# Attention scores as row-tiled matmuls, with the block mask added by 32-row matmuls, in a fused block-sparse attention and MLP kernel

## The chip, the cores and the metric

The kernel runs on one core of one Trainium2 chip. The metric is the device time of the launch in microseconds (us); lower is better. A run that is over 1.5% longer than the fastest run of the same kernel counts as slow and is left out of ratios. Ratios are computed as the mean time of one kernel's fast runs over the mean time of the other kernel's fast runs of the same rounds, so they are not quite the ratio of the medians quoted beside them.

The engines in the profile are PE (TensorE matmul), PEld (TensorE weight load), DVE (VectorE), ACT (ScalarE), POOL (GpSimd) and SP (SyncE, which here issues transfers). "PEclk" is the share of the full TensorE clock that was granted. PE computes with an array of 128 rows by 128 columns; a matmul can use a part of it, a tile, and the profile prints that part as rows*columns ("64*128").

## The reference, cut to what matters

Inputs q, k and v have the shape (4, 8, 768, 64): batch, heads, positions, head size. The keys are cut into 24 chunks of 32. For every query an upper bound of its score with each chunk is computed, the 6 best chunks that causality allows are kept, and all other scores are masked.

```python
ub = np.sum(np.maximum(q * k_min, q * k_max), axis=-1)      # shapes cut
ub = np.where(causal, ub, -1e9)
top_chunks = np.argsort(ub, axis=-1)[..., -6:]
scores = scale * np.matmul(q, k.transpose(0, 1, 3, 2))
mask = sel & (pos[:, None] >= pos[None, :])                 # sel: chunk of the key is among the 6
attn = softmax(np.where(mask, scores, -1e9))
x = np.matmul(attn, v)                                      # heads side by side: 3072 x 512
h = x @ w_in                                                # 512 -> 2048
out = elu(h) @ w_out                                        # 2048 -> 512
```

## The kernel before: the parts that matter here

Heads are worked on in 16 pairs (4 batches of 4 pairs). Queries 0 to 191 need no mask, since they have at most 6 chunks (Q0 = 192). A head has 64 numbers per key, so a score matmul needs only 64 of the 128 rows of the array. The kernel before uses the other 64 rows for the mask: rows that hold -40000 on "not selected" chunks are multiplied with a 0/1 selection. Score and mask are thus one 128-row matmul per head. The price is that K and Q of each head are copied to their own tiles (64 partitions each), and that the transposed selection, selT, must be moved to other partitions by four transfers per two pairs.

```python
for s in range(NSET):                       # NSET = 4, pairs t use set t % 4
    lhsA.append(const.tile([P, S], BF16))   # rows 0-63: K of head 0, rows 64-87: mask values
    lhsB.append(const.tile([P, S], BF16))   # rows 64-127: K of head 1, rows 0-23: mask values
    rhsA.append(const.tile([P, S], BF16))   # rows 0-63: Q of head 0, rows 64-87: selection
    rhsB.append(const.tile([P, S], BF16))
...
# prep(t): after PE has transposed K (and Q, in the same way)
nc.scalar.activation(out=lhsA[s][0:64, ts], in_=ps[0:64, :], func=AF.Copy)
nc.scalar.activation(out=lhsB[s][64:P, ts], in_=ps[64:P, :], func=AF.Copy)
...
# select(g): upper bounds of two pairs, thresholds, transposed selection
nc.vector.transpose(out=selT, in_=sb...)
for j in range(2):
    s = (2 * g + j) % NSET
    nc.sync.dma_start(out=rhsA[s][64:64 + NCH, Q0:S], in_=selT[64 * j:64 * j + NCH, :])
    nc.sync.dma_start(out=rhsB[s][0:NCH, Q0:S], in_=selT[64 * j + 32:64 * j + 32 + NCH, :])
...
# attend(t): 7 steps a pair, 9 score matmuls a head
for hd in range(2):
    sps = psS.tile([P, 512], F32, name="sps")            # psS: 2 PSUM banks
    for (kb, c0, w, pc) in segs:
        nc.tensor.matmul(sps[:, pc:pc + w], lhsT=lhs[hd][:, P * kb:P * (kb + 1)],
                         rhs=rhs[hd][:, c0:c0 + w], start=True, stop=True)
    nc.scalar.activation(out=pt[:, hd, 0:wtot], in_=sps[:, 0:wtot], func=AF.Exp, scale=SCALE)
# (steps of at most 256 columns put both heads in one bank and one exponential)
```

A scheduler orders each engine's instructions when the program is built; the MLP of one batch is filled in between the attention of the next. In program order loads of later pairs stand ahead of the selection's transfers in the SP queue.

The softmax here doesn't subtract the row's maximum and nothing guards it: scores larger than these inputs give would overflow.

## Time and profile before

| | before |
|---|---|
| time, median of 3 runs | 397.43 us (396.59 to 397.96) |
| profiled execution, first to last instruction | 394.6 us |
| mean granted clock | 0.930 |
| PE / ACT / DVE / POOL busy | 317.5 / 226.5 / 205.0 / 116.2 us |

The first lines are from the page of the kernel before: busy time per engine, and then the span in 40 slices (about 10 us each), each digit the busy share in tenths; the last line is the granted clock in tenths.

```profile
PE 317.5 (80%) x2272; PEld 175.1 (44%) x2272; DVE 205.0 (52%) x594; ACT 226.5 (57%) x489; POOL 116.2 (29%) x244
...
PE   1562068678869869999998788999999988979886
...
ACT  2633086696896894785378956672589143251430
...
PEclk9995559959998989999999699999999999999999
```

PE has a hole in the fifth slice (the "0"), is 60 to 90% busy while attention dominates, and is nearly full from the middle on. The clock falls to half around the hole and in a few slices after it. The first digits of the clock line mislead: the trace's clock records begin only 25.0 us into this span, and the 9s before them stand for no record. The fp32 transposes there start 213 ns apart, against 109 ns later at full clock, so PE ran at half clock.

The hole, from the timeline of the kernel before. Columns: start in us, duration in us, engine, source line, operation, what it writes and reads, count, and in brackets the engine's idle time before it and what ended it. "SPq" is the issue of a transfer from the SP queue.

```profile
28.02 0.77 DVE L214 STREAM_TRANSPOSE selT<-selb_171 128x576 bf16<-128x576 bf16 x1
...
31.59 9.38 SPq L85 DMA_DIRECT2D q_pair<-in_q_dram  x2
41.07 5.13 SPq L82 DMA_DIRECT2D k_pair<-in_k_dram  x2
46.30 0.86 SPq L217 DMA_DIRECT2D rhsA_119<-selT  x1
...
49.00 0.58 PE L243 MATMUL sps<-rhsA_119,lhsA_117 128*128 128x384 bf16 x2 [15.38 <-DMA rhsA_119<-selT]
```

The selection is ready at 28.8 us, but its transfer stands behind loads of later pairs and is issued at 46.3 us; PE waits 15.4 us for it, and the first score comes at 49.0 us.

One more reading: what a change of tiling mode costs, that is, of the part of the array that matmuls use. The kernel before has 16 such changes, around the upper-bound matmuls (ub), which write 64 columns of the array ("128*64") between ordinary 128*128 matmuls. Timeline, PE only:

```profile
63.50 0.34 PE L284 MATMUL pxt<-ident_b,on 128*128 128x128 bf16 x3
63.77 0.46 PE L200 MATMUL ub<-QTf,kst_133 128*64 128x288 f32 x1
63.78 0.46 PE L200 MATMUL ub<-QTf,kst_139 128*64 128x288 f32 x1
```

The spacing of starts is what counts, not the printed duration: a 384-column matmul is printed with about 0.32 us, but the next one can start 0.162 us after it. The third transpose starts at 63.621 us by the trace's own records; its 128 columns take 56 ns when such matmuls stand back to back; the next start is 150 ns after it. So 92 to 94 ns are lost, in six of the seven selections of the steady part.

### The profile page before, as it was taken

How to read it: one execution, taken by the hardware profiler on the slowest of the kernel's cores; microseconds unless marked ns; L12 is line 12 of the kernel's file. 1: busy time of each engine (PE TensorE's matmuls, PEld its weight loads, DVE VectorE, ACT ScalarE, POOL GpSimd, SP SyncE). 2: the span in 40 equal slices, each digit the busy share in tenths (PEclk: the TensorE clock that was granted, in tenths of full speed). 3: DMA queues.
4: the chain of work that ended last, by engine and by line, in shares of the span. 5: the costliest groups of instructions: out<-in, count | busy, mean ns of one | idle time of the engine just before them, and what ended most of it. 6: DMA issues, size and time to landing. Idle time of an engine off the chain costs nothing.

```text
span 394.6 us, 6477 instructions
## 1 busy us (share of the span) xinstructions
PE 317.5 (80%) x2272; PEld 175.1 (44%) x2272; DVE 205.0 (52%) x594; ACT 226.5 (57%) x489; POOL 116.2 (29%) x244
## 2 busy tenths in 40 slices
PE   1562068678869869999998788999999988979886
PEld 1331034444544545554555454554556444444442
DVE  7462026637638737555286396372686345252550
ACT  2633086696896894785378956672589143251430
POOL 7651001201413322243033233251133134151430
PEclk9995559959998989999999699999999999999999
DMA  9999993543643733930233034101100010200102
GB/s 174 209 186 189 192 207 21 85 108 24 87 104 21 113 81 26 173 94 2 80 28 26 2 26 54 53 2 45 38 13 2 27 53 2 80 2 35 44 2 80
DMA packets 82592, 27.52 MB, mean 70 GB/s; under 512 B 76160, under 2 KB 78976, under 8 KB 82560
## 3 DMA queue, kind: packets, MB, share of 16 engines
q1 hardware_dynamic: 54784, 19.77, 20.4%
q0 software_dynamic: 27776, 7.34, 18.2%
q8 instruction: 18, 0.29, 0.3%
q14 instruction: 14, 0.11, 0.1%
HBM read 27.26 MB, written 6.29 MB: 85 GB/s over the span
## 4 chain that ended last, share of the span: by engine, by line
issue 30%; PE 24%; ACT 18%; POOL 16%; DVE 8%; SPq 3%; DMA 1%; POOLq 0%; ACTq 0%
POOL m_sb L301 13%; PE o_ps L308 9%; ACT pt L246 5%; PE sps L243 4%; PE ub L200 3%; DVE gT L303 2%; PE h_ps L295 2%; SPq L85 2%; PE psK L162 2%; PE psQ L182 2%; ACT QTf L187 1%; SPq L82 1%; ACT e_sb L299 1%; ACT rhsB_120 L189 1%; ACT lhsB_118 L169 1%
## 5 line engine op out<-in xcount | busy, mean ns | idle before, releaser
L295 PE MATMUL h_ps<-xt,w_in_sb 128*128 128x384 bf16 x512 | 105.3, 327 | 12.1 <-DVE gT L303 11.5
L301 POOL TENSOR_SCALAR m_sb<-e_sb 128x384 f32<-128x384 f32 x128 | 65.6, 516 | 155.2 <-ACT e_sb L299 143.8
L246 ACT ACTIVATE pt<-sps 128x384 bf16<-128x384 f32 (+1 forms) x160 | 80.4, 534 | 53.4 <-PE sps L243 51.5
L303 DVE SCALAR_TENSOR_TENSOR gT<-h_ps,m_sb 128x384 bf16<-128x384 f32 x128 | 70.4, 554 | 41.4 <-POOL m_sb L301 38.1
L308 PE MATMUL o_ps<-w_out_sb,gT 128*128 128x512 bf16 x384 | 88.1, 379 | 0.0
L299 ACT ACTIVATE e_sb<-h_ps 128x384 f32<-128x384 f32 x128 | 62.3, 496 | 40.4 <-PE h_ps L295 38.6
L295 PEld LDWEIGHTS <-w_in_sb 128*128 128x128 bf16 x512 | 48.3, 97 | 47.3 <-issue 20.2
L308 PEld LDWEIGHTS <-gT 128*128 128x128 bf16 x384 | 37.2, 98 | 40.8 <-issue 1.0
L314 DVE COPY o_sb<-o_ps 128x512 f32<-128x512 f32 x16 | 11.1, 691 | 53.1 <-PE o_ps L308 53.0
L273 PEld LDWEIGHTS <-pt 128*128 128x128 bf16 x672 | 29.3, 103 | 17.5 <-DVE pt L255 8.0
L182 PE MATMUL psQ<-ident_f,q_pair 128*128 128x128 f32 x96 | 21.0, 338 | 17.3 <-ACT lhsB_118 L169 7.3
L162 PE MATMUL psK<-ident_f,k_pair 128*128 128x128 f32 x96 | 19.2, 317 | 11.2 <-DMA k_pair<-in_k_dram 4.6
L312 ACT ACTIVATE o_sb<-o_ps 128x512 f32<-128x512 f32 x8 | 4.8, 597 | 39.0 <-PE o_ps L308 39.0
L190 DVE TENSOR_SCALAR Qrl<-QTf 128x576 f32<-128x576 f32 x16 | 7.5, 469 | 35.1 <-ACT QTf L187 35.1
L182 PEld LDWEIGHTS psQ<-ident_f,q_pair 128*128 128x128 f32 x96 | 12.3, 164 | 28.5 <-ACT lhsB_118 L169 10.1
L243 PE MATMUL sps<-rhsA_119,lhsA_117 128*128 128x384 bf16 (+2 forms) x36 | 9.9, 315 | 18.4 <-DMA rhsA_119<-selT 15.4
L255 DVE TENSOR_TENSOR pt<-pt,tri_168 128x512 bf16<-128x512 bf16 x32 | 13.5, 421 | 13.4 <-ACT pt L246 13.4
L162 PEld LDWEIGHTS psK<-ident_f,k_pair 128*128 128x128 f32 x96 | 11.5, 157 | 19.6 <-ACT rhsB_120 L189 5.6
L249 ACT ACTIVATE pt<-sps 128x512 bf16<-128x512 f32 x32 | 19.3, 604 | 1.4 <-PE sps L243 1.3
L285 DVE COPY xt<-pxt 128x384 bf16<-128x384 bf16 x32 | 11.3, 352 | 16.2 <-PE pxt L284 15.8
L165 DVE TENSOR_REDUCE kmm<-psK 128x12 f32<-128x384 f32 x32 | 17.6, 549 | 3.9 <-PE psK L162 3.4
L166 DVE TENSOR_REDUCE kmm<-psK 128x12 f32<-128x384 f32 x32 | 17.4, 545 | 0.0
(220 smaller groups left out, 418.2 us busy)
## 6 DMA issues: line engine op xcount, KB each, us to landing
k_pair<-in_k_dram SPq DMA_DIRECT2D x32, 192.0 KB
q_pair<-in_q_dram SPq DMA_DIRECT2D x32, 192.0 KB
out_dram<-o_sb SPq DMA_DIRECT2D x24, 256.0 KB
w_in_sb<-in_moe_w_in_dram POOLq DMA_DIRECT2D x4, 512.0 KB, 8.9
w_out_sb<-in_moe_w_out_dram POOLq DMA_DIRECT2D x4, 512.0 KB, 17.3
vext_116<-in_v_dram POOLq DMA_DIRECT2D x8, 96.0 KB, 3.4
vext_122<-in_v_dram POOLq DMA_DIRECT2D x8, 96.0 KB, 3.6
vext_128<-in_v_dram POOLq DMA_DIRECT2D x8, 96.0 KB, 3.4
```

The costliest lines, as they stand in the source:

```text
L162: nc.tensor.transpose(ps[:, P * n:P * (n + 1)], k_pair[:, 3 * h + n], ident_f)
L165: nc.vector.tensor_reduce(out=kmm[:, 0, cs], in_=pv, axis=AX.X, op=AOT.min)
L182: nc.tensor.transpose(ps[:, P * n:P * (n + 1)], q_pair[:, 3 * h + n], ident_f)
L243: nc.tensor.matmul(sps[:, o + pc:o + pc + w], lhsT=lhs[hd][:, P * kb:P * (kb + 1)], rhs=rhs[hd][:, c0:c0 + w], start=True, stop=True)
L246: nc.scalar.activation(out=pt[:, hd, 0:wtot], in_=sps[:, 0:wtot], func=AF.Exp, scale=SCALE)
L249: nc.scalar.activation(out=pt[:, :, 0:256], in_=sps[:, :].rearrange("p (h w) -> p h w", h=2), func=AF.Exp, scale=SCALE)
L273: nc.tensor.matmul(o3[:, hd, qi, :], lhsT=pt[:, hd, P * qt + off:P * qt + off + P], rhs=vexts[s][:, kb, hd, :], start=(kb == 0), stop=(kb ...
L295: nc.tensor.matmul(hw, lhsT=w_in_sb[:, kk, P * fc:P * (fc + 1)], rhs=xT[NPAIR * b + kk][:, ts], start=(kk == 0), stop=(kk == NKK - 1))
L299: nc.scalar.activation(out=e_sb, in_=hw, func=AF.Exp)
L301: nc.gpsimd.tensor_scalar(out=m_sb, in0=e_sb, scalar1=-1.0, scalar2=1.0, op0=AOT.add, op1=AOT.mult)
L303: nc.vector.scalar_tensor_tensor(out=gT[:, fc, :], in0=hw, scalar=0.0, in1=m_sb, op0=AOT.max, op1=AOT.min)
L308: nc.tensor.matmul(o_ps, lhsT=gT[:, fc, P * tt:P * (tt + 1)], rhs=w_out_sb[:, fc, :], start=(fc == 0), stop=(fc == NFC - 1))
```

## The change

The intent: use the array's rows for two heads at once. The score matmul of head 0 uses rows 0 to 63 and that of head 1 rows 64 to 127, so both could run side by side; K and Q are then copied once with all 128 partitions. The mask becomes a second, accumulating matmul over the 32 rows in which the transposed selection already lies, so that its transfers go.

```diff
-    ptpool = pool("ptpool", 14)
+    ktpool = pool("ktpool", 5)
+    ptpool = pool("ptpool", 10)
-    xtpool = pool("xtpool", 12)
+    xtpool = pool("xtpool", 10)
 ...                                      # set-up of lhsA, lhsB, rhsA, rhsB goes; emask = econst
-            nc.scalar.activation(out=lhsA[s][0:64, ts], in_=ps[0:64, :], func=AF.Copy)
-            nc.scalar.activation(out=lhsB[s][64:P, ts], in_=ps[64:P, :], func=AF.Copy)
+            nc.scalar.activation(out=kT[t][:, ts], in_=ps, func=AF.Copy)
 ...                                      # the same for Q
-                for j in range(2):
+                for i in range(4):
+                    h, j = divmod(i, 2)
                     t = 2 * g + j
-                    nc.tensor.matmul(ub[64 * j:64 * j + 64, :], lhsT=kst[t % NSET][:, w, :],
+                    nc.tensor.matmul(ub[32 * i:32 * i + 32, :], lhsT=kst[t % NSET][:, w, h, :],
 ...
-        for j in range(2):
-            s = (2 * g + j) % NSET
-            nc.sync.dma_start(out=rhsA[s][64:64 + NCH, Q0:S], in_=selT[64 * j:64 * j + NCH, :])
-            nc.sync.dma_start(out=rhsB[s][0:NCH, Q0:S], in_=selT[64 * j + 32:64 * j + 32 + NCH, :])
+        selT_of[g] = selT
 ...
+                spss = [psS.tile([P, 512], F32, name="sps") for _ in range(2)]
+                for (kb, c0, w, pc) in segs:
+                    m0 = max(c0, Q0)
+                    for hd in range(2):
+                        hr = slice(64 * hd, 64 * hd + 64)
+                        nc.tensor.matmul(spss[hd][:, pc:pc + w], lhsT=kT[t][hr, P * kb:P * (kb + 1)],
+                                         rhs=qT[t][hr, c0:c0 + w], start=True, stop=False)
+                    for hd in range(2):
+                        mr = slice(64 * hd + 32 * (t % 2), 64 * hd + 32 * (t % 2) + 32)
+                        nc.tensor.matmul(spss[hd][:, pc + m0 - c0:pc + w],
+                                         lhsT=emask[mr, P * kb:P * (kb + 1)],
+                                         rhs=selT[mr, m0 - Q0:c0 + w - Q0], start=False, stop=True)
                 for hd in range(2):
 ...                                      # the shared exponential of small steps goes
+                    nc.scalar.activation(out=pt[:, hd, 0:wtot], in_=spss[hd][:, 0:wtot],
                                          func=AF.Exp, scale=SCALE)
```

More of the change, by code (lines that the diff above doesn't have):

```diff
@@ L97 @@
     nc.vector.tensor_copy(out=ident_b, in_=ident_f)
-    vexts, lhsA, lhsB, rhsA, rhsB, kst = [], [], [], [], [], []
+    vexts, kst = [], []
     for s in range(NSET):
         vexts.append(const.tile([P, NQT, 2, D + 1], BF16, name=f"vext{s}"))
-        lhsA.append(const.tile([P, S], BF16, name=f"lhsA{s}"))
-        lhsB.append(const.tile([P, S], BF16, name=f"lhsB{s}"))
-        rhsA.append(const.tile([P, S], BF16, name=f"rhsA{s}"))
-        rhsB.append(const.tile([P, S], BF16, name=f"rhsB{s}"))
-        kst.append(const.tile([P, 2, 64], F32, name=f"kst{s}"))
+        kst.append(const.tile([P, 2, 2, CHUNK], F32, name=f"kst{s}"))
     def load_v(t):
@@ L116 @@
         nc.vector.memset(vexts[s][:, :, :, D:D + 1], 1.0)
-        nc.vector.memset(rhsA[s][64:P, :], 0.0)
-        nc.vector.memset(rhsB[s][0:64, :], 0.0)
     econst = const.tile([P, NCH, CHUNK], BF16, name="econst")
     nc.vector.memset(econst, MASKNEG)
-    for r0 in (0, 64):
-        nc.gpsimd.affine_select(out=econst[r0:r0 + 64], in_=econst[r0:r0 + 64],
+    for r0 in range(0, P, 32):
+        nc.gpsimd.affine_select(out=econst[r0:r0 + 32], in_=econst[r0:r0 + 32],
                                 compare_op=AOT.is_equal, fill=0.0, base=0,
                                 pattern=[[1, NCH], [0, CHUNK]], channel_multiplier=-1)
-    for s in range(NSET):
-        nc.vector.tensor_copy(out=lhsA[s][64:P, :],
-                              in_=econst[64:P].rearrange("p c w -> p (c w)"))
-        nc.vector.tensor_copy(out=lhsB[s][0:64, :],
-                              in_=econst[0:64].rearrange("p c w -> p (c w)"))
+    emask = econst[:, :, :].rearrange("p c w -> p (c w)")
     tri01 = const.tile([P, P], BF16, name="tri01")
@@ L153 @@
     qf = {}
+    kT, qT = {}, {}
     def prep(t):
@@ L158, in prep @@
         kmm = smpool.tile([P, 2, NCH], F32, name="kmm")
+        kT[t] = ktpool.tile([P, S], BF16, name="kT")
+        qT[t] = ktpool.tile([P, S], BF16, name="qT")
         for h in range(2):
@@ L167, in prep @@
             ts = slice(HS * h, HS * (h + 1))
-            nc.scalar.activation(out=lhsA[s][0:64, ts], in_=ps[0:64, :], func=AF.Copy)
-            nc.scalar.activation(out=lhsB[s][64:P, ts], in_=ps[64:P, :], func=AF.Copy)
+            nc.scalar.activation(out=kT[t][:, ts], in_=ps, func=AF.Copy)
         for h in range(2):
             rows = slice(64 * h, 64 * h + 64)
-            cols = slice(32 * h, 32 * h + NCH)
-            nc.gpsimd.tensor_copy(out=kst[s][rows, 0, cols], in_=kmm[rows, 0, :])
-            nc.gpsimd.tensor_tensor(out=kst[s][rows, 1, cols], in0=kmm[rows, 1, :],
+            nc.gpsimd.tensor_copy(out=kst[s][rows, 0, h, 0:NCH], in_=kmm[rows, 0, :])
+            nc.gpsimd.tensor_tensor(out=kst[s][rows, 1, h, 0:NCH], in0=kmm[rows, 1, :],
                                     in1=kmm[rows, 0, :], op=AOT.subtract)
@@ L187, in prep @@
                 nc.scalar.activation(out=QTf[:, HS - Q0:], in_=ps, func=AF.Copy)
-            nc.scalar.activation(out=rhsA[s][0:64, ts], in_=ps[0:64, :], func=AF.Copy)
-            nc.scalar.activation(out=rhsB[s][64:P, ts], in_=ps[64:P, :], func=AF.Copy)
+            nc.scalar.activation(out=qT[t][:, ts], in_=ps, func=AF.Copy)
         nc.vector.tensor_scalar(out=Qrl, in0=QTf, scalar1=0.0, scalar2=None, op0=AOT.max)
+    selT_of = {}
     def select(g):
@@ L227, in attend @@
         s = t % NSET
-        lhs = (lhsA[s], lhsB[s])
-        rhs = (rhsA[s], rhsB[s])
+        selT = selT_of[t // 2]
         xt = xtpool.tile([P, S], BF16, name="xt")
@@ L236, in attend @@
                 pt = ptpool.tile([P, 2, 512], BF16, name="pt")
-                both = wtot <= 256
-                for hd in range(2):
-                    if not (both and hd == 1):
-                        sps = psS.tile([P, 512], F32, name="sps")
-                    o = 256 * hd if both else 0
-                    for (kb, c0, w, pc) in segs:
-                        nc.tensor.matmul(sps[:, o + pc:o + pc + w], lhsT=lhs[hd][:, P * kb:P * (kb + 1)],
-                                         rhs=rhs[hd][:, c0:c0 + w], start=True, stop=True)
-                    if not both:
-                        nc.scalar.activation(out=pt[:, hd, 0:wtot], in_=sps[:, 0:wtot],
-                                             func=AF.Exp, scale=SCALE)
-                if both:
-                    nc.scalar.activation(out=pt[:, :, 0:256],
-                                         in_=sps[:, :].rearrange("p (h w) -> p h w", h=2),
+                spss = [psS.tile([P, 512], F32, name="sps") for _ in range(2)]
[10 more added lines that the diff above has]
+                                         rhs=selT[mr, m0 - Q0:c0 + w - Q0], start=False, stop=True)
+                for hd in range(2):
+                    nc.scalar.activation(out=pt[:, hd, 0:wtot], in_=spss[hd][:, 0:wtot],
                                          func=AF.Exp, scale=SCALE)
```

## The prediction

> **What bounds it now.** No engine is full over the span (page, part 1: PE 80%, ACT 57%, DVE 52%, POOL 29%), but three stages differ. (1) Until 49 us the start: the timeline shows PE idle 33.6-49.0, waiting (list of waits: 15.4 us, the longest PE wait) for the copies of the transposed selection into rhsA/rhsB; they stand in the SP queue behind k/q loads and issue only at 46.3, though selT was ready at 28.8. (2) 49-307 us: attention with the MLP filled in. Counting a bf16 matmul at the spacing that the trace shows back to back (384 columns: 162 ns, 128: 56 ns, 65: about 30-40 ns), PE really streams some 185 of the 247 us from 60 to 307, about 75%; where the MLP is dense (170-200, 230-307) under 15% of PE's time is free, elsewhere 30-50%. (3) From 307 us MLP only, PE bound, untouched.
>
> **What the change does.**
> - Removes the mask copies and their wait: scores can start at about 30-33 us instead of 49. Worth about 15 us, if the freed time isn't lost to the k/q loads of the next pairs.
> - ACT: 128 copies of 64x384 (0.48 us each) become 64 of 128x384: -31 us. The 32 merged exponentials (604 ns) become 64 of 256 columns, estimated 0.40 us from the 332/491/604 ns of 192/384/512 columns: +6 us. Net -25 of 226 us. ACT isn't the limit, so little of it shows.
> - PE: every score matmul gets a second, 32-row one. Tiling saves time only if the two heads run side by side; but both score buffers (psS, 2) are freed one at a time, and the instruction order of the changed kernel shows the scheduler mostly emitting head 0 score, head 0 mask, head 1 score, head 1 mask: I count 20 score-score and 32 mask-mask neighbours of 288 possible each. So the mask streams 2432 columns x 2 heads x 16 = 77,800 columns, +32 us on PE.
> - Mode changes: about 710 between 128-row, 64-row and 32-row matmuls in that order. The Trainium skill ("TensorEngine Tiling (Array Packing)", Key Properties) says that changing the tiling mode drains TensorE. This trace agrees for column tiles: between the xt transposes (128x128) and ub (128x64) there are 92 ns beyond the streaming in six of seven selections, and about 95 ns on leaving. 710 x 0.092 = +65 us, an estimate: no row tile is in this trace.
> - ub in four 32-column tiles instead of two of 64: same time. Fewer pt and xt buffers: small loss.
>
> **On the critical path.** PE gains about 97 us of work against some 63 us of idle in stage 2, which is itself mostly waiting between scores and exponentials. One head's fill grows from 0.16 to about 0.5 us, as long as the exponential (0.49), so the two-buffer ping-pong slows from about 1.0 to 1.3-1.4 us a step. Filling stage 2 to 80-88% gives +53 to +84 us; less 15 at the start: about +50.
>
> **Prediction:** 448 us, range 408 to 495. Faster by over 2%: 0.08; within 2%: 0.10; slower by over 2%: 0.82.
>
> **What would show it.** Score start near 30 us and no PE wait on a DMA of selT; ACT busy near 202 us; 576 score and mask matmuls; gaps of about 90 ns at each score/mask change with no semaphore wait; PE releasing ACT's exponentials later; the MLP tail unchanged at some 87 us but later.
>
> **What would make it wrong.** Row-tile changes costing nothing (then about 405), or heads overlapping although other work stands between; the start gaining more than 15 us; ACT relief being worth more than I think; or a drain plus exposed weight load nearer 200 ns (then 490 or more).

## The result, and the profile after

The changed kernel is correct and takes 487.82 us (median of 3 runs, 486.53 to 495.22). The ratio of its fast runs to those of before is 1.228 (95% interval 1.221 to 1.235): slower by 23%. The execution profiled first fell in the slow state (495.2 us, clock 0.78). So it was profiled once more, at 488.09 us, in line with its fast runs; all lines below are from that second profile.

> The changed kernel once more, for a profile that isn't of the slow state (the first profile fell in it, at 495 us). Every theory: 486 to 490 us, clock near 0.79, the same gaps at the mode changes.

That expectation held: 488.09 us, clock 0.795.

The page's lines that answer to those of before:

```profile
PE 455.4 (94%) x2676; PEld 214.5 (44%) x2688; DVE 202.0 (42%) x578; ACT 207.6 (43%) x457; POOL 118.0 (24%) x246
...
PE   4699999999999999999999999999999999898986
...
ACT  3353445354557436533445544624434441515150
...
PEclk9955655655599989995756889996755569999999
```

PE now looks full from the third slice until the MLP tail. But the clock line is at 5 and 6 tenths in about half of the slices in which attention runs. A PE that reads "9" there streams at half the pace: 384 columns take 0.32 us instead of 0.16, as the lines below show.

The start, PE only, answers to the hole of before:

```profile
23.69 0.26 PE L236 MATMUL sps<-selT,econst 32*128 32x192 bf16 x2
23.88 0.23 PE L232 MATMUL sps<-qT,kT 64*128 64x128 bf16 x2
```

The first mask matmuls run at 23.7 us instead of the first scores at 49.0: the queued transfers no longer hold them up, and the start gained 25 us. About 6 us of it is that the selection itself is ready earlier (selT at 22.9 us instead of 28.8). The first two score matmuls need no selection any more and stand at 10.8 us already, but their exponentials wait for the masks, until 24.9 us.

The same kernel's score (64*128) and mask (32*128) matmuls of 384 columns, first at full clock and, two microseconds later, at half clock (the trace's clock records put the step in this stretch):

```profile
53.67 0.33 PE L232 MATMUL sps<-qT,kT 64*128 64x384 bf16 x1
53.94 0.33 PE L236 MATMUL sps<-selT,econst 32*128 32x384 bf16 x1
...
55.97 0.50 PE L232 MATMUL sps<-qT,kT 64*128 64x384 bf16 x1
56.40 0.50 PE L236 MATMUL sps<-selT,econst 32*128 32x384 bf16 x1
56.83 0.50 PE L232 MATMUL sps<-qT,kT 64*128 64x384 bf16 x1
```

At full clock the mask starts 0.27 us after its score, although 384 columns need 0.162 us where nothing changes: about 0.1 us is the change of mode. At half clock it is 0.43 us: 0.32 of streaming and about 0.11 of change. There is no bracket, hence no semaphore wait, on these lines. Head 0's score, head 0's mask, head 1's score and head 1's mask follow each other, as the instruction order had shown; the two heads mostly do not run side by side. In the trace 17 score pairs and 32 mask pairs of 144 each start within 15 ns of each other.

The waits view (engine, line, what it waited for: us in total, times, longest). Exponentials that wait for scores, and scores that wait for exponentials, in the kernel before:

```profile
ACT pt L246 <- PE sps L243: 51.5, 27, 16.9
PE sps L243 <- ACT pt L246: 11.2, 18, 2.3
```

The same two in the changed kernel:

```profile
ACT pt L240 <- PE sps L236: 134.3, 127, 5.1
PE sps L232 <- ACT pt L240: 2.4, 5, 0.7
```

ACT now waits for PE, and PE hardly ever for ACT. So relieving ACT from 226.5 to 207.6 us can be worth little here.

To put the 92 us of difference in places, I added up the starts of all matmuls in both traces: streaming at the spacing seen back to back at full clock (162 ns per 384 bf16 columns and 109 ns per 128 fp32 columns, in proportion; side-by-side matmuls once), the extra time that the half clock puts on this streaming (with the start, before the first clock record, at half clock), up to 115 ns at each change of tiling mode, and the rest as idle. The four add up to the span, apart from 8 to 9 us of start and end. It is arithmetic on the trace, not a view of the profile. The trace of the changed kernel lacks 12 matmul records of the MLP, which counts some 2.6 us too much as idle.

| us | before | changed | difference |
|---|---|---|---|
| streaming at full clock | 262.8 | 289.3 | +26.5 |
| half clock on that streaming | 16.8 | 76.8 | +60.0 |
| gaps at changes of mode (16 and 712) | 1.6 | 75.2 | +73.6 |
| PE idle | 104.7 | 36.6 | -68.1 |
| span | 394.6 | 486.4 | +91.8 |

PE's idle time took up 68 of the 160 us that were added; the half clock is the term that the prediction did not have.

The windows view shows where. Columns: stretch in us, its length, then busy us and count of instructions per engine, the granted clock, the DMA share, GB/s. The kernel before, from 20 us to its MLP tail:

```profile
20.00:120.00 100.00, 63.30 (x489) 36.31 (x489) 45.10 (x155) 62.48 (x135) 21.00 (x46) 0.78 0.73 118
120.00:220.00 100.00, 90.13 (x706) 50.70 (x706) 61.77 (x191) 69.66 (x154) 31.70 (x70) 0.98 0.38 63
220.00:307.00 87.00, 81.68 (x658) 46.28 (x657) 51.21 (x152) 59.76 (x132) 25.29 (x52) 0.96 0.13 26
307.00:395.00 88.00, 75.72 (x404) 37.55 (x400) 34.24 (x61) 25.85 (x52) 25.05 (x50) 0.99 0.09 37
```

The changed kernel:

```profile
20.00:120.00 100.00, 93.50 (x519) 42.04 (x517) 38.83 (x132) 44.24 (x101) 16.16 (x37) 0.57 0.66 103
120.00:220.00 100.00, 98.03 (x674) 48.34 (x677) 49.50 (x143) 51.70 (x119) 25.71 (x57) 0.93 0.35 64
220.00:320.00 100.00, 97.93 (x613) 47.72 (x616) 47.34 (x137) 46.38 (x105) 26.67 (x55) 0.80 0.15 19
320.00:400.00 80.00, 79.64 (x434) 32.17 (x434) 24.66 (x77) 32.95 (x69) 7.65 (x15) 0.64 0.02 7
400.00:487.00 87.00, 74.69 (x380) 36.94 (x381) 33.20 (x58) 26.25 (x53) 25.00 (x49) 0.99 0.10 37
```

The last line of each is the MLP alone, 87 to 88 us with the same work in both: untouched. The loss is all in the part with attention. Where little MLP work stands between (20 to 120 and 320 to 400 us) the clock is 0.57 and 0.64 with PE over 93% "busy".

### The profile page after: what moved, and what is told of

Its sections match the earlier page's. It is cut to its first block, busy times and chain, and to the rows that moved or that the text cites. A ratio compares the mean times of both kernels' runs of the same rounds, so it can differ in the third digit from the quotient of the medians.

```text
span 493.5 us, 7230 instructions
## 1 busy us (share of the span) xinstructions
PE 461.9 (94%) x2676; PEld 215.6 (44%) x2688; DVE 202.3 (41%) x578; ACT 208.0 (42%) x457; POOL 117.9 (24%) x246
## 4 chain that ended last, share of the span: by engine, by line
PE 53%; issue 28%; POOL 10%; DMA 4%; SPq 2%; ACT 2%; DVE 1%; POOLq 0%; ACTq 0%
PE sps L232 11%; PE sps L236 10%; POOL m_sb L291 9%; PE o_ps L298 8%; PE h_ps L285 8%; DMA q_pair<-in_q_dram 4%; PE ub L194 3%; PE psQ L174 3%; PE psK L156 3%; PE pxt L274 1%; ACT pt L240 1%; SPq L86 1%; SPq L83 1%; DVE gT L293 0%; PE o_2732 L263 0%
## 5 line engine op out<-in xcount | busy, mean ns | idle before, releaser
L240 ACT ACTIVATE pt<-sps 128x384 bf16<-128x384 f32 (+2 forms) x224 | 106.4, 491 | 140.1 <-PE sps L236 138.8
L285 PE MATMUL h_ps<-xt,w_in_sb 128*128 128x384 bf16 x512 | 122.0, 364 | 9.9 <-DVE gT L293 9.6
L232 PE MATMUL sps<-qT,kT 64*128 64x384 bf16 (+2 forms) x288 | 99.2, 364 | 2.7 <-ACT pt L240 2.4
L236 PE MATMUL sps<-selT,econst 32*128 32x384 bf16 (+3 forms) x288 | 90.1, 345 | 0.0
L232 PEld LDWEIGHTS <-kT 64*128 64x128 bf16 x288 | 26.0, 96 | 64.8 <-issue 58.1
L236 PEld LDWEIGHTS <-econst 32*128 32x128 bf16 x288 | 24.7, 96 | 53.2 <-issue 44.9
L263 PEld LDWEIGHTS <-pt 128*128 128x128 bf16 x672 | 38.4, 119 | 19.2 <-issue 14.3
L156 PE MATMUL psK<-ident_f,k_pair 128*128 128x128 f32 x96 | 22.3, 361 | 5.4 <-DMA k_pair<-in_k_dram 4.6
L159 DVE TENSOR_REDUCE kmm<-psK 128x12 f32<-128x384 f32 x32 | 17.7, 552 | 21.9 <-PE psK L156 21.7
L162 ACT ACTIVATE kT<-psK 128x384 bf16<-128x384 f32 x32 | 15.6, 491 | 22.9 <-DVE kmm L160 22.9
```

The source lines that it names most:

```text
L156: nc.tensor.transpose(ps[:, P * n:P * (n + 1)], k_pair[:, 3 * h + n], ident_f)
L159: nc.vector.tensor_reduce(out=kmm[:, 0, cs], in_=pv, axis=AX.X, op=AOT.min)
L232: nc.tensor.matmul(spss[hd][:, pc:pc + w], lhsT=kT[t][hr, P * kb:P * (kb + 1)], rhs=qT[t][hr, c0:c0 + w], start=True, stop=False)
L236: nc.tensor.matmul(spss[hd][:, pc + m0 - c0:pc + w], lhsT=emask[mr, P * kb:P * (kb + 1)], rhs=selT[mr, m0 - Q0:c0 + w - Q0], start=False, ...
L240: nc.scalar.activation(out=pt[:, hd, 0:wtot], in_=spss[hd][:, 0:wtot], func=AF.Exp, scale=SCALE)
L263: nc.tensor.matmul(o3[:, hd, qi, :], lhsT=pt[:, hd, P * qt + off:P * qt + off + P], rhs=vexts[s][:, kb, hd, :], start=(kb == 0), stop=(kb ...
```

## The experiments

The edits shown are cut and shortened to what matters.

Theory A: the changes of tiling mode cost about 0.1 us each, and the half clock belongs to what the change does on PE; both together make the loss. Rival B: the loss comes from the doubled number of score matmuls, their extra streaming, and the slower filling of the two score buffers; mode changes matter little. For the half clock there are two candidates of its own: it follows the number of mode changes (empty gaps), or it follows how little of the array 64-row and 32-row matmuls use.

All ratios below are to runs of the kernel before on the same chip in the same rounds. "Changes" are the mode changes counted in the trace.

| run | time, us (median) | ratio to before, 95% | clock of the profiled run | changes | gaps / half clock / idle, us |
|---|---|---|---|---|---|
| all 128 rows | 391.03 | 0.984 (0.980 to 0.988) | 0.982 | 16 | 2 / 9 / 74 |
| mask over 64 rows | 385.43 | 0.969 (0.965 to 0.972) | 0.990 | 364 | 36 / 6 / 45 |
| before + 32-row one-column | 443.16 | 1.115 (1.110 to 1.119) | 0.884 | 586 | 61 / 33 / 76 |
| before + 128-row one-column | 399.60 | 1.006 (1.004 to 1.008) | 0.923 | 16 | 2 / 18 / 108 |
| changed, heads paired | 424.98 | 1.070 (1.067 to 1.072) | 0.904 | 601 | 62 / 31 / 44 |
| all 128 rows + 32-row one-column | 428.09 | 1.078 (1.075 to 1.081) | 0.984 | 589 | 59 / 9 / 54 |
| mask over 64 rows, heads paired | 399.84 | 1.005 (1.001 to 1.009) | 0.932 | 439 | 44 / 21 / 48 |
| before, selection placed directly | 389.69 | 0.981 (0.977 to 0.984) | 0.952 | 16 | 2 / 17 / 97 |
| all 128 rows + more one-column | 442.08 | 1.112 (1.104 to 1.119) | 0.973 | 715 | 73 / 12 / 53 |
| mask over 64 rows, 3 score banks | 411.61 | 1.039 (1.033 to 1.045) | 0.987 | 324 | 32 / 7 / 81 |

One run of "mask over 64 rows" (389.6 us) and one of "all 128 rows + more one-column" (446.7 us) counted as slow and are not in the ratios. All ten results are correct: the edits keep the arithmetic.

### All 128 rows: the same matmuls, no mode changes

```diff
-  nc.tensor.matmul(spss[hd][:, pc:pc + w], lhsT=kT[t][hr, P * kb:...], rhs=qT[t][hr, c0:c0 + w], ...)
+  nc.tensor.matmul(spss[hd][:, pc:pc + w], lhsT=kT[t][:, P * kb:...], rhs=qz[s][hd][:, c0:c0 + w], ...)
-  lhsT=emask[mr, ...], rhs=selT[mr, ...]
+  lhsT=emk[hd][t % 2][:, ...], rhs=selT[:, ...]     # zeros outside the 32 rows
```

> The changed kernel with every score and mask matmul over 128 rows (zeros in the other head's q rows and in the other masks' rows), so the same 576 matmuls in the same kind of order but only 16 mode changes instead of 712; 32 more copies of 64x384 on ACT (+16 us of ACT). Theory A (mode changes, about 0.1 us each, and the half clock that comes with them, cost most of the +90 us): 390 to 415 us, clock above 0.9, almost no gaps at the mask matmuls. Rival B (twice as many score matmuls, 28 us more streaming and the slower fill of two score buffers cost it): 450 to 490 us.

It took 391.03 us, at the low end of Theory A's range and far from Rival B's. With 297 us of streaming, more than the changed kernel's 289, it is even a little faster than the kernel before. So the extra streaming and the split of score and mask cost nothing net: PE's idle time and the earlier start pay for them. Rival B has fallen. The variant also keeps the changed kernel's smaller buffer pools, its four ub tiles and its separate exponentials, so these are not the cause either. Its clock line:

```profile
PEclk9995899999999999999999999999999999999999
```

### The mask over 64 rows: half of the mode changes

```diff
+  emk = [const.tile([P, S], BF16, name=f"emk{j}") for j in range(2)]   # zero, but rows 32j and 64+32j on
-  mr = slice(64 * hd + 32 * (t % 2), 64 * hd + 32 * (t % 2) + 32)
+  mr = slice(64 * hd, 64 * hd + 64)
-  lhsT=emask[mr, P * kb:P * (kb + 1)],
+  lhsT=emk[t % 2][mr, P * kb:P * (kb + 1)],
```

> The changed kernel with the mask matmul over 64 rows (the other pair's 32 mask rows are zero), the same mode as its score matmul: 364 mode changes by the instruction order instead of 712, the same streaming. Theory A: some 35 us of gaps go and part of the clock comes back: 430 to 455 us, clock 0.83 to 0.9. Rival B: 480 to 490 us, as the changed kernel.

Outside both ranges, and better than either theory said: 385.43 us, 3% faster than the kernel before and 21% faster than the changed kernel (385.43/487.82 = 0.79), from one constant and one slice. Counting changes alone would give about 40 us. The other gain is the clock, 0.99: by the sum, half clock is 6 us instead of 77. Its clock line:

```profile
PEclk9988999999999999999999999999999999999999
```

Its timeline at full clock, with no gap between score and mask:

```profile
69.14 0.32 PE L237 MATMUL sps<-qT,kT 64*128 64x384 bf16 x1 [0.57 <-ACT pt L245]
69.30 0.32 PE L241 MATMUL sps<-selT,emk 64*128 64x384 bf16 x1
```

The mask follows its score after 0.16 us, the streaming time of 384 columns, instead of 0.27 us. This fits the Trainium skill, "TensorEngine Tiling (Array Packing)", Key Properties, which says that changing the mode, not just the tile, drains the array.

### Mode changes put into the kernel before, and their control

```diff
+  nc.tensor.matmul(sps[:, o + pc:o + pc + 1], lhsT=econst_f[0:32, P * kb:P * (kb + 1)],
+                   rhs=tri01[0:32, 0:1], start=True, stop=True)      # control: rows 0:P
   nc.tensor.matmul(sps[:, o + pc:o + pc + w], lhsT=lhs[hd][:, P * kb:P * (kb + 1)], ...)
```

> The kernel before with a one-column 32-row matmul ahead of each score matmul (its result is overwritten by the score): 586 mode changes, next to no added streaming, all real streaming still over 128 rows. Theory A: gaps of 0.1 us each add some 58 us to PE, part of it taken from idle time: 425 to 460 us; and if the changes themselves bring the clock down, clock below 0.87. If instead the clock falls because 64- and 32-row matmuls count as little work, the clock stays above 0.91 and the time near 420 to 430. Rival B: within 2% of the one-column 128-row control.

> Control for the run before it: the same one-column matmul, over 128 rows, so no mode changes but the same 288 extra weight loads and matmuls. Every theory: 397 to 408 us, clock 0.92 to 0.94.

The control took 399.60 us and the 32-row version 443.16 us. So 288 small matmuls cost 2 us, and making them 32 rows tall costs 44 us more: 570 changes at 76 ns each net. By the sum, gaps add 60 us (0.1 us each) and half clock 15 us, and 31 us come out of idle time. That mode changes by themselves cost time is shown. The clock came out between the two bounds that I had set (0.884), so this pair alone does not decide what lowers it. The clock lines of the control and of the 32-row version:

```profile
PEclk9985559968999969999999689999999999999999
...
PEclk9975556665995995999999869999999999999999
```

### The changed kernel with the heads side by side

```diff
+  # NoSync ordering edge: mask matmul of head 0 behind the score matmul of head 1
+  tc.add_manual_dep(mask_of_head_0, score_of_head_1.name, NoSync)
```

> The changed kernel with one ordering edge more: the first head's mask matmul is issued after the second head's score matmul, so that heads stand side by side as the change meant (by the instruction order 131 of 144 mask pairs and 68 of 144 score pairs are neighbours). 601 mode changes instead of 712, some 20 us less streaming. Theory A (mode changes and the clock): gaps near 60 us, clock between that of the changed kernel and 0.9: 430 to 465 us. If lost side-by-side running were the whole cause: 390 to 405 us.

It took 424.98 us, 5 us below the range of Theory A: with the pairing that the change had in mind it is 63 us faster than the changed kernel, and still 7% slower than the kernel before. Pairing helps in three ways at once (streaming 280 us instead of 289, where some 20 us less were expected; 111 fewer changes; clock 0.904), so it is no clean test of one of them; but it shows that lost side-by-side running is not the whole cause.

### What lowers the clock: mode changes, or few rows?

```diff
+  # between score and mask of the all-128-row variant: one column, zeros, 32 rows
+  nc.tensor.matmul(spss[hd][:, pc + m0 - c0:pc + m0 - c0 + 1], lhsT=zero_b[0:32, :],
+                   rhs=tri01[0:32, 0:1], start=False, stop=False)
```

> The all-128-row variant (391 us, clock 0.98) with a one-column 32-row matmul of zeros between score and mask: 589 mode changes, all real streaming over 128 rows. If mode changes bring the clock down by their number: clock 0.80 to 0.90, gaps near 60 us, 435 to 475 us. If the clock falls because 64- and 32-row matmuls count as little work: clock above 0.93 and 405 to 430 us.

The time, 428.09 us, is 37 us over the all-128-row variant, with 59 us of gaps. The clock did not move: 0.984 against 0.982. So here 589 mode changes with their empty gaps do not bring the half clock. That cannot be said of all 128-row streaming: the 586 changes put into the kernel before, which streams fewer columns, did take its clock from 0.923 to 0.884. The sum below reconciles the two. The follow-up sets as many changes as the changed kernel has, by one more such matmul ahead of the score of key block 0:

```diff
+  if kb == 0:
+      nc.tensor.matmul(spss[hd][:, pc:pc + 1], lhsT=zero_b[0:32, :], rhs=tri01[0:32, 0:1],
+                       start=True, stop=True)
```

> The all-128-row variant with one-column 32-row matmuls put in until it has 715 mode changes by the instruction order, as many as the changed kernel (712); the same masks and scores stream, but over 128 rows. If the half clock follows the share of array rows that are fed in each stretch (a sum over the traces so far: after a stretch of 3.4 us with under about 0.37 of the array's full-speed work the clock is halved): clock above 0.95, gaps near 72 us, 435 to 455 us. If it follows the number of mode changes: clock near 0.8 and 480 to 495 us.

It took 442.08 us at a clock of 0.973, with 715 changes and 73 us of gaps against 712 and 75 us in the changed kernel. Its windows up to the MLP tail, to be held against those of the changed kernel:

```profile
20.00:120.00 100.00, 90.01 (x736) 51.97 (x736) 45.79 (x154) 57.82 (x133) 20.19 (x47) 0.88 0.71 112
120.00:220.00 100.00, 96.56 (x789) 53.48 (x791) 50.49 (x153) 52.79 (x120) 26.12 (x54) 1.00 0.34 58
220.00:320.00 100.00, 98.27 (x782) 55.19 (x785) 52.18 (x158) 55.32 (x126) 24.80 (x54) 1.00 0.14 23
320.00:355.00 35.00, 34.79 (x324) 20.14 (x322) 15.26 (x38) 21.23 (x48) 6.13 (x12) 1.00 0.01 1
```

PE is as busy as in the changed kernel, but the clock is 0.88 and then 1.00, where the changed kernel has 0.57, 0.93, 0.80 and 0.64. With the same number of changes and gaps, 128-row scores and masks instead of 64- and 32-row ones are worth 46 us (488 less 442), although this variant even has 352 small matmuls and 32 more ACT copies. So the number of changes does not set the half clock; the few rows in use bring it here.

A sum over all thirteen traces supports this. Each was cut into stretches of 3.413 us along the steps in the trace's clock records, from the first record on (1,507 stretches, of which 257 are followed by half clock). In each, the columns that every matmul streams (feeds) were added up, weighted by its share of the array's rows and columns, as a share of what full streaming would give. An fp32 column counts twice, since it takes twice the time (109 against 56 ns per 128). The clock of the next stretch was half exactly when this share was under 0.37, in all but 12 stretches. The 0.37 was on record before three of these traces were taken; in those, 5 of 370 are wrong. Other rules do worse even at their best cut: without the weighting 74 are wrong, by PE's busy time 216, by the number of mode changes 255, and "the clock stays as it is" is wrong 115 times. With fp32 columns counted once, 0.37 is wrong 62 times, so the rule leans on that choice. It is a fit and covers data of this one kernel family only.

The same sum reconciles the two pairs above. Between 20 and 120 us the mean share is 0.38 in the 128-row control and 0.30 in the 32-row version: the gaps push a share near the cut below it. In the all-128-row variant it is 0.65, with 589 changes 0.54 and with 715 changes 0.48, all above; in the changed kernel 0.28. Empty gaps and few rows both lower the share.

The rule fits with single pairs: a 384-column score and mask at 64 and 32 rows feed (384 x 64 + 384 x 32)/128 = 288 full columns, 0.12 us worth, in 0.53 us: a share of 0.23, and at half clock, in 0.86 us, 0.14. Only other work in the same 3.4 us can lift it over 0.37; that fits the clock's recovery in the stretches that are dense with MLP. In the variant just shown, two 256-column matmuls over 128 rows take 0.52 us with two changes of mode: 0.21/0.52, a share of 0.41.

### The heads side by side in one mode

This is the 64-row mask with the ordering edge of the paired variant.

> The 64-row mask variant (385 us) with the same ordering edge: both heads side by side in one mode, some 30 us less streaming, but 439 mode changes instead of 364 by the order. Theory A: streaming gain about cancels 75 changes of 0.1 us unless the clock gives way: 372 to 388 us. If changes past some density bring the half clock back: 390 to 415 us.

It took 399.84 us, worse than without the edge. It has 439 changes instead of 364 (waiting for both score buffers may let other work in between; not tested), streams 276 us instead of 286, and the clock falls to 0.932; its clock line shows where:

```profile
PEclk9975565589999999999999999999999999999999
```

Between about 20 and 90 us, where there is little MLP work yet, the clock is mostly at half. So pairing can lose: here it moved the total up by 14 us. How much of this is clock (21 us by the sum, against 6) and how much order is not separated further.

### The kernel before with only its start mended

```diff
-  nc.tensor.matmul(ub[64 * j:64 * j + 64, :], lhsT=kst[t % NSET][:, w, :], ...)
+  h, j = 1 - i // 2, i % 2            # four 32-column tiles, so that selT lands on the right rows
+  nc.tensor.matmul(ub[32 * i:32 * i + 32, :], lhsT=kst[t % NSET][:, w, h, :], ...)
-  nc.sync.dma_start(out=rhsA[s][64:64 + NCH, Q0:S], in_=selT[64 * j:64 * j + NCH, :])   # and rhsB
+  nc.gpsimd.tensor_copy(out=rh[s][r0:r0 + 32, Q0:S], in_=selT[r0:r0 + 32, :])
```

> The kernel before with only the start mended: the selection is laid out so that its transposed rows already stand on the partitions that the masks need, and POOL copies replace the queued transfers; no row tiles. If the earlier start is what the change gained: scores start at about 29 us instead of 49 and the time is 372 to 385 us. If the later pairs' loads take the gain back: 393 to 398 us.

It took 389.69 us, between the two expectations: the score start moved to 36.5 us, not 29, since the order that the scheduler made now has the selection later (selT is ready at 35.7 us instead of 28.8). The gain of 7 us over the kernel before comes with no row tile at all. At the 2% mark its verdict is unclear, but the interval (0.977 to 0.984) is clear of no change. So an earlier start is a gain of its own here, and of the 12.5 us only a part arrives at the end. The edit also changes the ub tiles and adds POOL copies, which are not separated from it.

### A third score buffer

```diff
-  psS = pool("psS", 2, ...); psM = pool("psM", 3, ...)
+  psS = pool("psS", 3, ...); psM = pool("psM", 2, ...)      # in the variant with the mask over 64 rows
```

> The 64-row mask variant (385 us) with a third score buffer, taken from the MLP's three: 324 mode changes by the instruction order instead of 364. 4 us fewer gaps and less waiting for exponentials, against fewer MLP buffers in the last 87 us: 376 to 392 us; the open question is only whether it beats 385.

A miss: 411.61 us. The bank was taken from the MLP. The last 88 us, by the windows view, first of the variant with three MLP banks (294 to 382 us) and then of this one:

```profile
294.00:382.00 88.00, 75.97 (x389) 37.51 (x387) 34.06 (x60) 26.90 (x54) 25.53 (x50) 0.99 0.09 37
320.00:408.00 88.00, 63.50 (x301) 29.43 (x303) 27.54 (x48) 21.90 (x44) 21.07 (x42) 1.00 0.07 27
```

PE is busy 63.5 us instead of 76.0, with 301 matmuls instead of 389: the tail is stretched, and a good part of the 26 us is lost there, with 40 fewer changes and the same clock. How much was lost earlier is not separated.

## Why the prediction was right, and where its sum was off

The prediction forecast slower by over 2% (448 us, range 408 to 495), and 487.82 us is in the range. The direction and the two costs that it named, masks and mode changes, are confirmed. That the time lies near the upper end of the range is no credit to its sum: the terms that it had, as measured, add up to +32 us, some 429 us, and the rest is the half clock, which it did not have. Point by point:

- "scores can start at about 30-33 us instead of 49": right in kind, and larger. The first mask matmul is at 23.7 us, in part because the selection is ready 6 us earlier; the wait for the queued transfers is gone.
- "ACT [...] Net -25 of 226 us [...] little of it shows": right. ACT is 207.6 us, 19 less, and waits 134.3 us for scores.
- "the mask streams [...] +32 us on PE": right; measured +26.5 us, some masks being side by side. The all-128-row variant shows that this term, taken with the earlier start, costs nothing in the end.
- "about 710 [mode changes]" at "0.092": right; 712 in the trace, with 75.2 us of gaps instead of 65. Row tiles cost about as much as the column tiles from which the estimate was taken, about 90 to 110 ns. The one-column experiment shows the cost by itself: 44 us net for 570 changes.
- "PE gains about 97 us of work": measured 26.5 + 73.6 = 100 us. This was right almost to the number, the streaming being some 6 us under and the gaps some 9 us over the estimate.
- "the two-buffer ping-pong slows from about 1.0 to 1.3-1.4 us a step": this is not what set the pace. PE's waits for exponentials fell from 11.2 to 2.4 us; PE itself was the limit.
- "Filling stage 2 to 80-88% gives +53 to +84 us; less 15 at the start: about +50": this is the step that came out too small. Idle time took up 68 us, more than I had assumed (97 - 50 = 47); so the sum without another term would have been +32 us. The term left out was the clock: it was taken to stay as it was, and fell from 0.93 to 0.795, 60 us by the sum, 46 us by the variant that has as many changes over 128 rows. That makes +92.
- "a drain plus exposed weight load nearer 200 ns (then 490 or more)" was the reason that I gave in advance for a time near 490. It was not that reason; the gap stayed near 0.1 us. That the time came near 490 all the same is chance.

Put as a ladder of medians: before 397; scores and masks split but over 128 rows 391; the same with 589 changes of mode 428 and with 715 changes 442; as many changes with 64 and 32 rows, the changed kernel, 488. The rungs differ in small things besides, named above, but the two large steps, +51 for changes of mode and +46 for few rows, are each an experiment of its own. That PE's clock follows the share of the array that is fed, and not something else that goes with it in these kernels, is supported by the fit, not proved.

The Trainium skill's remark in "Perfetto Trace Analysis", Identifying the Most-Contended Engine, that matmul busy share is a bad measure of how close PE is to its limit, agrees: PE went from 80% to 94% busy, while the full-clock streaming went from 67% (262.8 of 394.6) to 59% (289.3 of 486.4) of the span.

## What to carry to other kernels

In this kernel row tiling paid only where neighbours on PE mostly kept the same mode: count the changes in the order that the scheduler really makes, and price each at about 0.1 us, as measured here. If two tile heights meet, try padding the smaller one with zeros to the larger one's mode; here a mask over 64 rows instead of 32 turned 488 us into 385, which beat both kernels. And look at the clock line beside the busy line: here PE was over 93% busy with 64- and 32-row matmuls and the gaps between them, at 0.57 of its clock.

## What the Trainium skill lacked or had wrong

- "TensorEngine Tiling (Array Packing)", Key Properties: says that a change of mode drains the array, and gives no figure. Here each change, in either direction and for row tiles as for column tiles, cost about 90 to 110 ns beyond the streaming at full clock, and 712 of them 75 us.
- The same page, When to Use Tiling: advises 4x row tiling for a contraction of 32, without a warning there for a stream that also has 64-row matmuls. Here 32 rows gave 488 us and the same mask over 64 rows 385 us.
- "TensorE: Matmul & The Clock Gate", Part 1: the clock has a full and a half state, set over windows of 3.4 us by how busy PE has been. The states (1.0 and 0.5) and the window (steps in the clock records are 3.413 us or multiples) agree. Its advice to "Keep TensorE busy ≥4µs continuously" (in "Why this matters for your kernels") was not enough here: with PE 93 to 100% busy the clock was 0.57 and 0.64 over stretches of 80 to 100 us. What fitted was the share of array rows and columns fed, with a cut at about 0.37 (12 of 1,507 stretches wrong); no page has this.
- No page has that pairing row tiles may lower the clock: the paired 64-row variant had 0.932 and 400 us, the unpaired 0.990 and 385 us.
